# Seven of 24 attention chunks: q, k and x turned by DMAs from SBUF to SBUF instead of TensorE transposes and PSUM copies

## The chip, the cores and the metric

The kernel runs on one core of a Trainium2 chip. The time is device time in microseconds (us) of one execution. Three executions of the kernel before gave 196.27, 196.29 and 194.94 us, median 196.27. Besides, one execution was profiled; it took 197.9 us.

A core has TensorE (PE, with its weight loads shown as PEld), VectorE (DVE), ScalarE (ACT), GpSimd (POOL) and SyncE (SP), each with its own queue of instructions in a fixed order. TensorE writes into eight PSUM banks, which are emptied by DVE or ACT. DMAs move data between HBM and SBUF, or within SBUF; here all of them are issued by SP and run on 16 DMA engines.

## The reference, cut to what matters

A gated linear attention with a recurrent state, for 4 batches of 8 heads with 768 steps and a head size of 48, feeds a two-layer MLP with a squared ReLU:

```python
for t in range(S):
    state = alpha[:, :, t, :, None] * state + einsum('bhd,bhe->bhde', k[:, :, t], v[:, :, t])
    y[:, :, t] = einsum('bhd,bhde->bhe', q[:, :, t], state)
x = y.transpose(0, 2, 1, 3).reshape(3072, 384)
r = maximum(x @ w_in, 0.0)          # w_in 384 x 2048
out = (r * r) @ w_out               # w_out 2048 x 384
```

## The kernel before, in words

The 3072 tokens are 24 chunks of 128 (six per batch; a chunk of the code is `s`, its place in the batch `c`). For each chunk:

- SP loads alpha, q, k and v (L299), 192 KB each, in pieces of 192 bytes. A weight load is L264, a result's store L549.
- ACT takes the logarithm of alpha into `L_s` (L321). PE multiplies it by a triangle of ones, which gives the prefix sums (`e_p0`). ACT makes A = exp(sums) and Ainv = exp(-sums) (L340, L344) and two small decays `ae_s` (L347, L350).
- DVE makes qA_s = q * A (L359) and kI_s = k * Ainv (L362), bf16, heads padded from 48 to 64 so that two heads fill 128 columns. There are four slots of them.
- PE transposes qA_s and kI_s into a PSUM bank, four 128x128 transposes each (`e_p1q`, `e_p1k`; the helper `tr` is L224, all other matmuls are L221), and DVE copies the bank into `qkT` (`e_cp`, `cast`, L316).
- PE makes the scores `sc` from qkT (`e_p2`, 8 matmuls), DVE masks them into `sm` (L400, two halves). PE updates the state `st` (`e_ps`), DVE decays it (L420), ACT casts it to `sb` (L425).
- PE adds the part of the former state (`e_p3a`, from qkT and sb) and of the chunk itself (`e_p3b`, from sm and vb); ACT casts the bank to `xn` (L314). PE transposes xn in three blocks (`e_p4`, L224), and DVE copies them into `xT_big` (`e_xT`, L316).

The MLP runs on groups of chunks: 4, 1, 1 and then nine groups of 2. For a group, up-projection matmuls read xT_big and w_in_b, ACT applies ReLU (L504), DVE squares into `gT` (L512). Down-projection matmuls read gT and w_out_b, 16 for each chunk in four quarters; ACT or DVE copies the sum to `ob` (L544 or L542) and SP stores it.

The order of all of this is set before the kernel runs by a small planner (`Plan`). Each step is an `Op` with an engine, a cost in us, the steps it depends on, a latency until its result can be used, and the PSUM banks it takes. The planner goes through time, starts on each engine what can start first, and sorts by start. Instructions are then emitted in that order and kept in it (`pin`, `keep_in_program_order`), so every engine's queue, SP's among them, has a fixed order, and an instruction that waits holds all behind it on its engine. A store is put into the order 3.5 us after its data are planned to be there (`OUT_LATE`). `LEAD` keeps the attention some chunks ahead of the MLP, so that between the steps of a chunk PE has up- and down-projection matmuls of earlier groups.

Loads have six buffers each, `qkT`, `xn` and `sm` four.

Of the kernel before, what the change touches and what calls it, by code (L numbers as in the profile page):

```python
# [9 lines left out]
BF16 = mybir.dt.bfloat16  # L10
# [44 lines left out]
def after(op, x=0.0):  # L55
    return (op, x)
# [83 lines left out]
def kernel(  # L140
# [10 lines left out]
    nc = tc.nc  # L151
    B, H, S, D = q.shape
    HD = H * D
    P = 128
    DP = 64
    NP = H // 2
# [17 lines left out]
    big = ctx.enter_context(tc.tile_pool(name="big", bufs=1))  # L174
    LB = 6
    loads = ctx.enter_context(tc.tile_pool(name="loads", bufs=LB))
    work = ctx.enter_context(tc.tile_pool(name="work", bufs=4))
# [17 lines left out]
        out=utri_f, in_=utri_f, compare_op=ALU.is_ge, fill=0.0,  # L195
# [10 lines left out]
    NBUF = 4  # L206
    L_s = big.tile([P, NBUF, H, DP], BF16)
    nc.gpsimd.memset(L_s[:, :, :, D:], 0.0)
    qA_s = big.tile([P, NBUF, H, DP], BF16)
    nc.gpsimd.memset(qA_s[:, :, :, D:], 0.0)  # L210
    kI_s = big.tile([P, NBUF, H, DP], BF16)
    nc.gpsimd.memset(kI_s[:, :, :, D:], 0.0)
    ae_s = big.tile([P, NBUF, NP, 2], FP32)
    nc.vector.memset(ae_s, 0.0)  # L214
    xT_big = big.tile([P, KT, n_tok], BF16)

    def pin(ins):
        tc.keep_in_program_order(ins)
# [4 lines left out]
    def tr(*a):  # L223
        pin(nc.tensor.transpose(*a))  # L224

    plan = Plan()
# [4 lines left out]
    GLA_BANKS = sl_bank[0:2]  # L231
# [11 lines left out]
    def add(eng, dur, emit, *deps, **kw):  # L243
        return plan.add(Op(eng, dur, emit, deps, **kw))
# [43 lines left out]
    state = {}  # L288
    SRC = dict(srcs)
    EARLY = 4  # L290

    def add_load(s, nm):
        d = C[s]
        b, c = divmod(s, NCH)

        def ld():
            if nm not in d:
                d[nm] = loads.tile([P, H, D], FP32, name=nm)
            pin(nc.sync.dma_start(out=d[nm], in_=SRC[nm][b, c]))  # L299
        prev = C[s - LB]["use_" + nm] if s >= LB else None  # L300
        d["ld_" + nm] = add("DMA", LD, ld, prev, lat=2.0 if s < 4 else 2.4, at=0.8)

    def add_chunk(s):
        d = C[s]
        b, c = divmod(s, NCH)
        i = s % NBUF
        L, qA, kI, ae = L_s[:, i], qA_s[:, i], kI_s[:, i], ae_s[:, i]
        old = C[s - NBUF].get("end") if s >= NBUF else None
        g = dict(prio=-10.0 + s * 0.01)
        last = c == NCH - 1  # L310

        def cast(op, out_t, in_t):
            if op.eng == "ACT":
                pin(nc.scalar.copy(out_t, in_t))  # L314
            elif op.eng == "DVE":
                pin(nc.vector.tensor_copy(out_t, in_t))  # L316
            else:
                pin(nc.gpsimd.tensor_copy(out_t, in_t))

        def e_ln():  # L320
            pin(nc.scalar.activation(L[:, :, 0:D], d["at"], AF.Ln))  # L321
        ln = d["use_at"] = add("ACT", 0.41, e_ln, d["ld_at"], old, prio=-15.0 if s < EARLY else -5.0)

# [39 lines left out]
        mq = d["use_qt"] = add("DVE", 0.47, e_qA, a_, d["ld_qt"], old, **g)  # L363
        mk = d["use_kt"] = add("DVE", 0.47, e_kI, ai, d["ld_kt"], old, **g)
# [6 lines left out]
        def e_p1k():  # L371
            for p in range(NP):
                tr(d["pT"][:, NP + p, :], kI[:, 2 * p:2 * p + 2, :], ident_bf)
        p1q = plan.add(Op("PE", 0.22, e_p1q, [mq], takes=GLA_BANKS, **g))
        p1k = plan.add(Op("PE", 0.22, e_p1k, [mk, after(p1q)], lat=0.15, **g))

        def e_cp(lo, hi):
            if lo == 0:
                d["qkT"] = work.tile([P, 2 * NP, P], BF16, name="qkT")
            cast(cpk if lo else cp, d["qkT"][:, lo:hi, :], d["pT"][:, lo:hi, :])  # L380
        if s < EARLY:
            cp = add({"ACT": 0.49, "DVE": 0.34}, 0, lambda: e_cp(0, NP), p1q, **g)
            cpk = add({"DVE": 0.34, "ACT": 0.49}, 0, lambda: e_cp(NP, 2 * NP), p1k, after(cp, -9.0), **g)
        else:
            cp = cpk = add("DVE", 0.61, lambda: e_cp(0, 2 * NP), p1k, **g)
        p1q.gives = cpk

        def e_p2():
            sc = d["sc"] = ps_sc.tile([P, 2, NP, P], FP32, name="sc")
# [60 lines left out]
        xn = add("ACT", 0.36, e_xn, p3b, **g)  # L450
        (p3a or p3b).gives = xn

        def e_p4():
            d["px"] = psum(p4, [P, KT, P], BF16)
            for j in range(KT):
                tr(d["px"][:, j, :], d["xn"][:, j * P:(j + 1) * P], ident_bf)
        p4 = plan.add(Op("PE", 0.165, e_p4, [xn], takes=GLA_BANKS, lat=0.14, **g))

        def e_xT():
            cast(xT, xT_big[:, :, s * P:(s + 1) * P], d["px"])  # L460
        xT = add({"ACT": 0.36, "DVE": 0.27} if s < EARLY else "DVE", 0.27, e_xT, p4, prio=-9.0)
        d["x"] = d["end"] = xT
        p4.gives = xT

    GN = [4, 1, 1, 2, 2, 2, 2, 2, 2, 2, 2, 2]
    assert sum(GN) == NT
# [88 lines left out]
    for d in DMA_ORDER + [s for s in range(NT) if s not in DMA_ORDER]:  # L555
        if d in ("i", "o"):
            load_w(d)
        else:
            for s, nm in LOAD_ORDER.get(d, [(d, nm) for nm, _ in srcs]):
                add_load(s, nm)  # L560
            if d == 3:
                add_chunk(2)
            if d != 2:
                add_chunk(d)
# [83 lines left out]
```

## Time and profile before

| what | value |
|---|---|
| median of three executions | 196.27 us (194.94 to 196.29) |
| the profiled execution | 197.9 us, its span 196.2 us, mean granted TensorE clock 0.991 |
| PE busy | 183.9 us, 94% of the span |
| DVE, ACT, POOL busy | 130.0, 122.4, 16.3 us |
| weight loads (PEld) busy | 133.3 us |
| DMA packets of SP's queue | 107408, 29.89 MB, 74.1% of 16 engines' span |
| chain of waits by engine | PE 75%, SP's queue 9%, DMA 8%, DVE 4% |

The span is cut into 40 slices of 4.9 us; a digit is the busy share of a slice in tenths, 9 being 90% or more. Rows of groups name the line, the engine, the operation, what it writes and reads, the shapes, and how often. The chain of waits is followed back from the last instruction: at each step to what released it, or to the instruction before it on its engine. "To landing" is the time from the issue of a DMA on SP to the arrival of its data. The granted clock of PE was 1.00 after the first 45 us; before that it was 0.50 in one stretch of some 3.4 us (39.0 to 42.4 us).

### The profile page before, as it was taken

The numbers are of one execution on the slowest core, as the hardware profiler recorded it, in microseconds if no ns is written. First come the engines' busy times: TensorE is split into PE (matmuls) and PEld (weight loads), VectorE is DVE, ScalarE is ACT, GpSimd is POOL, SyncE is SP. The second block draws the span as 40 slices with busy tenths as digits, with TensorE's granted clock in tenths as the row PEclk, the third lists the DMA queues.
The fourth block names the chain that finished last, engine by engine and source line by source line (L and its number), as shares of the span: only waits on it lengthen the run. The fifth ranks groups of instructions, "written<-read, shape, count | busy, mean of one in ns | idle before, by whom it ended". The sixth has DMA issues, their size and how long they took to land.

```text
span 196.2 us, 4979 instructions
## 1 busy us (share of the span) xinstructions
PE 183.9 (94%) x1958; PEld 133.3 (68%) x1959; DVE 130.0 (66%) x277; ACT 122.4 (62%) x291; POOL 16.3 (8%) x37
## 2 busy tenths in 40 slices
PE   7888799599979999999999999999999999999991
PEld 2566554256768787867877877867868868768660
DVE  0688897725599797985786866858758767734200
ACT  3465688323988686875956856956955845718210
POOL 5110100011103021111111100110110000000000
PEclk9999999969999999999999999999999999999999
DMA  6999999999999999999999999871100110111111
GB/s 124 190 188 152 301 383 373 196 255 175 225 251 180 153 198 201 175 191 193 222 191 209 201 177 235 158 164 40 40 35 10 38 45 5 40 40 43 39 60 62
DMA packets 107431, 30.20 MB, mean 154 GB/s; under 512 B 100368, under 2 KB 106256, under 8 KB 107408
## 3 DMA queue, kind: packets, MB, share of 16 engines
q1 hardware_dynamic: 107408, 29.89, 74.1%
q8 instruction: 15, 0.25, 0.5%
q14 instruction: 8, 0.07, 0.1%
HBM read 25.17 MB, written 4.72 MB: 152 GB/s over the span
## 4 chain that ended last, share of the span: by engine, by line
PE 75%; SPq 9%; DMA 8%; DVE 4%; issue 1%; ACT 0%
PE bank L221 65%; SPq L299 8%; PE bank L224 6%; DMA wo<-in_moe_w_out_dram 4%; DMA wi<-in_moe_w_in_dram 4%; PE sc L221 3%; PE st L221 1%; DVE w_in_b L270 1%; DVE gT L512 1%; DVE sm L400 1%; SPq L264 1%; DVE w_out_b L270 0%; DVE qkT L316 0%; DVE kI_s L362 0%; ACT A L340 0%
## 5 line engine op out<-in xcount | busy, mean ns | idle before, releaser
L221 PE MATMUL bank<-xT_big,w_in_b 128*128 128x256 bf16 (+3 forms) x587 | 76.1, 270 | 0.3 <-ACT r L504 0.2
L221 PE MATMUL bank<-w_out_b,gT 128*128 128x384 bf16 x384 | 73.1, 331 | 2.2 <-DVE w_out_b L270 2.2
L504 ACT ACTIVATE r<-bank 128x512 bf16<-128x512 f32 (+2 forms) x100 | 57.5, 585 | 19.5 <-PE bank L221 16.8
L221 PEld LDWEIGHTS <-w_in_b 128*128 128x128 bf16 x588 | 49.6, 97 | 10.6 <-DVE w_in_b L270 0.5
L221 PEld LDWEIGHTS <-gT 128*128 128x128 bf16 x384 | 35.5, 99 | 22.6 <-issue 4.0
L512 DVE TENSOR_TENSOR gT<-r 128x512 bf16<-128x512 bf16 (+2 forms) x100 | 39.0, 416 | 13.9 <-ACT r L504 13.7
L400 DVE TENSOR_TENSOR sm<-sc,utri_b 128x512 bf16<-128x512 f32 x48 | 30.8, 684 | 2.9 <-PE sc L221 2.9
L544 ACT COPY ob<-bank 128x384 f32<-128x384 f32 x24 | 11.6, 482 | 25.1 <-PE bank L221 25.0
L359 DVE TENSOR_TENSOR qA_s<-qt,A 128x384 bf16<-128x384 f32 x24 | 13.3, 554 | 20.0 <-ACT A L340 20.0
L326 POOL CAST vb<-vt 128x384 bf16<-128x384 f32 x24 | 13.5, 563 | 129.3 <-DMA vt<-in_v_dram 74.7
L316 DVE COPY qkT<-bank 128x1024 bf16<-128x1024 bf16 (+1 forms) x28 | 17.1, 614 | 9.6 <-PE bank L224 9.4
L321 ACT ACTIVATE L_s<-at 128x384 bf16<-128x384 f32 x24 | 12.5, 522 | 8.2 <-DMA at<-in_alpha_dram 8.1
L221 PEld LDWEIGHTS <-qkT 64*128 64x128 bf16 (+1 forms) x272 | 10.8, 95 | 6.8 <-issue 2.1
L340 ACT ACTIVATE A<-bank 128x384 bf16<-128x384 f32 x24 | 12.0, 498 | 4.9 <-PE bank L221 4.8
L314 ACT CAST xn<-bank 128x384 bf16<-128x384 f32 x24 | 11.5, 480 | 5.2 <-PE bank L221 5.1
L362 DVE TENSOR_TENSOR kI_s<-kt,Ainv 128x384 bf16<-128x384 f32 x24 | 13.9, 579 | 0.3 <-DMA kt<-in_k_dram 0.3
L425 ACT CAST sb<-st 128x384 bf16<-128x384 f32 x20 | 9.5, 476 | 6.2 <-DVE st L420 6.0
L221 PE MATMUL bank<-warm 128*128 128x256 bf16 (+1 forms) x59 | 11.0, 317 | 1.3 <-DVE ae_s L214 1.3
L344 ACT ACTIVATE Ainv<-bank 128x384 bf16<-128x384 f32 x24 | 12.0, 500 | 0.0
L420 DVE TENSOR_TENSOR st<-st,ae_s 128x384 f32<-128x384 f32 x20 | 11.2, 558 | 0.2 <-PE st L221 0.2
L224 PE MATMUL bank<-ident_bf,kI_s 128*128 128x128 bf16 x96 | 9.3, 219 | 1.7 <-DVE qkT L316 1.7
L221 PE MATMUL bank<-vb,sm 128*128 128x48 bf16 x192 | 9.5, 184 | 1.2 <-DVE sm L400 0.7
(38 smaller groups left out, 130.4 us busy)
## 6 DMA issues: line engine op xcount, KB each, us to landing
at<-in_alpha_dram SPq DMA_DIRECT2D x24, 192.0 KB, 4.5
qt<-in_q_dram SPq DMA_DIRECT2D x24, 192.0 KB, 4.6
kt<-in_k_dram SPq DMA_DIRECT2D x24, 192.0 KB, 4.4
vt<-in_v_dram SPq DMA_DIRECT2D x24, 192.0 KB, 4.3
out_dram<-ob SPq DMA_DIRECT2D x24, 192.0 KB, 2.9
wo<-in_moe_w_out_dram SPq DMA_DIRECT2D x4, 768.0 KB, 8.7
wi<-in_moe_w_in_dram SPq DMA_DIRECT2D x3, 768.0 KB, 7.6
wi<-in_moe_w_in_dram SPq DMA_DIRECT2D x2, 384.0 KB, 5.7
```

Source lines behind the costliest of these rows:

```text
L221: pin(nc.tensor.matmul(*a, **kw))
L224: pin(nc.tensor.transpose(*a))
L299: pin(nc.sync.dma_start(out=d[nm], in_=SRC[nm][b, c]))
L316: pin(nc.vector.tensor_copy(out_t, in_t))
L321: pin(nc.scalar.activation(L[:, :, 0:D], d["at"], AF.Ln))
L326: pin(nc.gpsimd.tensor_copy(d["vb"], d["vt"]))
L340: pin(nc.scalar.activation(d["A"], d["pm"][:, 0:HD].rearrange("p (h d) -> p h d", h=H), AF.Exp))
L359: pin(nc.vector.tensor_mul(qA[:, :, 0:D], d["qt"], d["A"]))
L362: pin(nc.vector.tensor_mul(kI[:, :, 0:D], d["kt"], d["Ai"]))
L400: pin(nc.vector.tensor_mul(d["sm"][:, hh], d["sc"][:, hh], utri_b.to_broadcast([P, NP, P])))
L504: pin(nc.scalar.activation(box["r"][:, 0:w], box["ph"][:, 0:w], AF.Relu))
L512: pin(nc.vector.tensor_mul(gT[g][:, f0:f0 + per, lo * P:lo * P + n], r, r))
```

## The change

From chunk 17 on, qA_s and kI_s of a chunk, which now lie side by side in one tile `qk_s`, are transposed into qkT by one DMA from SBUF to SBUF on SP's queue, and xn is transposed into xT_big by another. The transposes on PE, their PSUM banks and the DVE copies are left out for these chunks. The planner gets a new engine "XB" for the two steps, with costs of 0.8 and 0.5 us and a latency of 2.0 us; this only sets the order, since both are issued by SP. Chunks 0 to 16 are as before.

```diff
-    qA_s = big.tile([P, NBUF, H, DP], BF16)
+    qk_s = big.tile([P, NBUF, 2, H, DP], BF16)
+    qA_s, kI_s = qk_s[:, :, 0], qk_s[:, :, 1]
     nc.gpsimd.memset(qA_s[:, :, :, D:], 0.0)
-    kI_s = big.tile([P, NBUF, H, DP], BF16)
     nc.gpsimd.memset(kI_s[:, :, :, D:], 0.0)
...
+    XFROM = 17
...
-        p1q = plan.add(Op("PE", 0.22, e_p1q, [mq], takes=GLA_BANKS, **g))
-        p1k = plan.add(Op("PE", 0.22, e_p1k, [mk, after(p1q)], lat=0.15, **g))
+        if s < XFROM:
+            p1q = plan.add(Op("PE", 0.22, e_p1q, [mq], takes=GLA_BANKS, **g))
+            p1k = plan.add(Op("PE", 0.22, e_p1k, [mk, after(p1q)], lat=0.15, **g))
...
-        if s < EARLY:
+        def e_turn():
+            d["qkT"] = work.tile([P, 2 * NP, P], BF16, name="qkT")
+            pin(nc.sync.dma_start_transpose(out=d["qkT"], in_=qk_s[:, i].rearrange("p x h d -> p (x h d)")))
+        if s >= XFROM:
+            cp = cpk = add("XB", 0.8, e_turn, mq, mk, lat=2.0, **g)
+        elif s < EARLY:
...
-        p1q.gives = cpk
+        if s < XFROM:
+            p1q.gives = cpk
...
-        p4 = plan.add(Op("PE", 0.165, e_p4, [xn], takes=GLA_BANKS, lat=0.14, **g))
+        if s < XFROM:
+            p4 = plan.add(Op("PE", 0.165, e_p4, [xn], takes=GLA_BANKS, lat=0.14, **g))
...
-        xT = add({"ACT": 0.36, "DVE": 0.27} if s < EARLY else "DVE", 0.27, e_xT, p4, prio=-9.0)
+        def e_xturn():
+            pin(nc.sync.dma_start_transpose(out=xT_big[:, :, s * P:(s + 1) * P], in_=d["xn"]))
+        if s < XFROM:
+            xT = add({"ACT": 0.36, "DVE": 0.27} if s < EARLY else "DVE", 0.27, e_xT, p4, prio=-9.0)
+            p4.gives = xT
+        else:
+            xT = add("XB", 0.5, e_xturn, xn, lat=2.0, prio=-9.0)
         d["x"] = d["end"] = xT
-        p4.gives = xT
```

## The prediction

> **What bounds the kernel now.** I read the page first, then the busy times by stretch, then the chain of waits in order of time, then the timeline of one chunk, and last the DMA queue around the place of the change. In the page's slices, two rows matter: PE, and the share of the DMA engines.
>
> ```profile
> PE   7888799599979999999999999999999999999991
> ...
> DMA  6999999999999999999999999871100110111111
> ```
>
> A slice is 4.9 us. PE is full from slice 13 to the last but one. The DMA engines are full up to slice 25 (123 us), at 8 and 7 tenths in the next two, and nearly empty from 132 us. Chunk 17's kI_s, the first product that the change sends through a DMA, ends at 126.97 us (DVE row of L362, start 126.42 us, 0.55 us), just where the loads run out. The stretch from there to the last chunk's x is this one (columns: stretch, length, busy us of PE, PEld, DVE, ACT and POOL with counts, granted clock, DMA share, GB/s):
>
> ```profile
> 126.00:176.00 50.00, 50.00 (x547) 37.52 (x545) 34.62 (x75) 31.54 (x78) 1.59 (x3) 1.00 0.18 50
> ```
>
> PE is busy 50.00 of 50.00 us at full clock and the view of waits lists none for it here. DVE and ACT have a third of their time left. So time taken off PE's queue here is time off the end, as long as no new wait takes its place. The chain of waits says how much the transposes hold (start, length, what):
>
> ```profile
> 161.30 0.17 PE bank L224 x3
> 161.47 0.65 PE bank L221 x4
> 162.12 0.45 PE bank L224 x8
> 162.57 0.17 PE st L221 x4
> 162.74 0.98 PE bank L221 x9
> 163.72 0.33 PE sc L221 x8
> ```
>
> L224 is the transpose helper: 3 matmuls for x of one chunk (0.17 us of the chain), 8 for q and k of the next (0.45 us, elsewhere as two times 0.22). Last, what a transposed chunk waits for today, from the timeline (start, length, instruction):
>
> ```profile
> 159.58 0.32 PE L221 MATMUL bank<-L_s,utri_b 128*128 128x384 bf16 x1
> ...
> 161.34 0.55 DVE L362 TENSOR_TENSOR kI_s<-kt,Ainv 128x384 bf16<-128x384 f32 x1
> ...
> 162.60 0.69 DVE L316 COPY qkT<-bank 128x1024 bf16<-128x1024 bf16 x1 [0.45 <-PE bank L224]
> ...
> 163.65 0.40 PE L221 MATMUL sc<-qkT 64*128 64x128 bf16 x8
> ```
>
> The prefix sums (L_s) start at 159.58 us, kI_s is done at 161.89 us, the scores (sc) start at 163.65 us: 1.76 us from kI_s to the scores now.
>
> **What it removes.** Seven chunks (17 to 23) lose 4+4+3 transposes each. On the chain 0.17+0.45 = 0.61 to 0.62 us a chunk, so 7 x 0.61 = 4.3 us off PE. This is the whole possible gain: -4.3 us. (The busy times of the 77 matmuls add to 7.23 us, but they overlap each other; the chain's share counts.) DVE loses 7 qkT copies of 0.69 and 7 xT copies of 0.35 us, 7.3 us: costed at nothing, since DVE's 15.4 us of idle time in the stretch hide it; no wait of PE's ends in it, so without that cover there would still be no gain. Two PSUM banks come free sooner; no wait here is for a bank: nothing. q and k now share one tile, with the same memsets: nothing.
>
> **What it adds.** Per chunk two DMAs on SP's queue: q and k together (128x1024 bf16, 256 KB), x (128x384, 96 KB). By their output shapes (128x8x128, 128x3x128) I count 1024 and 384 pieces of 256 B, 64 and 24 for each of 16 DMA engines. No row shows such a DMA. Its neighbours are loads (1024 pieces of 192 B) and results (128 pieces of 1536 B), issue to landing. In the stretch where the loads run out, and in the quiet one after it:
>
> ```profile
> qt<-in_q_dram SPq DMA_DIRECT2D x1, 192.0 KB, 2.9
> kt<-in_k_dram SPq DMA_DIRECT2D x1, 192.0 KB, 3.5
> vt<-in_v_dram SPq DMA_DIRECT2D x1, 192.0 KB, 3.7
> ```
>
> ```profile
> out_dram<-ob SPq DMA_DIRECT2D x10, 192.0 KB, 1.9
> ```
>
> The lower end is 1.9 us. The upper is the median of loads in a crowd, 4.4 us (page, kt). I take 2.9 us: qt had the rings almost to itself and has the 64 pieces per engine that q and k have, while kt and vt, issued 0.5 and 1.1 us behind it, queued on it. With 0.03 us from a finished producer to SP's issue (ob ends at 160.05, its result is issued at 160.08 us) and some 0.1 us (estimate of the same kind) to PE, the way from kI_s to the scores is L = 3.03 us; ends 2.0 and 4.5.
>
> **Who waits for it.** PE runs in a fixed order, so scores that are late hold everything behind them. The changed order puts them later. Counting what PE does from a chunk's prefix sums to its scores in that order (three up-projection matmuls 0.33, four down-projection 0.65, scores 0.33, state 0.17, p3a 0.17, p3b 0.21, prefix sums 0.26 us, all from the timeline): 5.7, 6.0, 5.6, 5.7, 5.4, 5.7, 5.6 us for chunks 17 to 23. From prefix sums to the end of kI_s the trace takes 2.3 us (159.58 to 161.89), or 2.5 where a ReLU lies between (166.74 to 169.27); I take 2.4. The rooms for L are 3.3, 3.6, 3.2, 3.3, 3.0, 3.3, 3.2 us, 22.9 in sum. At L = 3.03 nothing waits but chunk 17: its DMA stands behind qt of chunk 23 in the rings, which was issued at 126.53 and landed 2.9 us later, at 129.4 us. Then come 64 pieces per engine at 21.7 ns (74.1% of 16 engines' 196.2 us over 107408 packets), 1.4 us, so 130.8 us against 126.97+3.3 = 130.3: +0.6 us with the hop.
>
> Moved on SP: chunk 17's transpose stands ahead of kt and vt of chunk 23, which are needed 30 us later; x of chunks 19 and 21 stands ahead of q and k of 20 and 22, issued some 0.3 us before kI_s is done (p3b starts 1.08 us after the prefix sums, xn ends 1.05 us later, kI_s at 2.4), and 24 pieces at 21.7 ns, 0.5 us, go first: 0.15 us each, +0.3 us. Results between them have left ACT long before (they are ordered 3.5 us late). x itself: xn ends some 1.05 us after its chunk's p3b starts (159.38 to 160.43 us), and from p3b to the group's first up-projection PE has 5.0 us of work for chunk 17 (whose x stands behind q and k of 18) and 4.1 to 4.3 us for 19, 21 and 23: rooms of 3.9 and 3.1 to 3.2 us. Its landing lies between the result's 1.9 and qt's 2.9 us, so nothing; if it took 4.4 us, about 1.3 us for each of three groups.
>
> **The sum.** -4.3 +0.6 +0.3 = -3.4 us. The profiled execution took 197.9 us, 1.7 us more than its span of 196.2; by the sum it would take 194.5 us. The three runs shown have a median of 196.27 us, 0.8% below it; the terms are differences within the span, so I set them against this median: 192.9 us.
>
> [...] The row: SP needs 0.33 us for a result's issue and 0.37 us for qt's. [...]
>
> **Rivals.**
> *Slower, SP's issue or the crossbar is slow.* If a transpose lands later than the scores' turn, PE stands still in each chunk. For: SP's longest issue of a load took 2.51 us (vt at 121.98); against: that one met full rings. With 2.5 us of issue and the 1.6 us that a result needs after its issue, L = 4.2: six chunks wait 6 x 4.2 - 19.6 = 5.6, chunk 17 waits 0.9, x ahead of q and k costs 0.6 twice. -4.3+7.7 = +3.4 us, 199.7 us. The loads in a crowd, L = 4.5, give +8.6-4.3, 200.6 us. It decides from 6L - 19.6 + 0.6 = 4.3, L = 3.9 us.
> *A wash.* L of 3.5 to 4.1 us (kt's and vt's 3.5 and 3.7 us are such rows): waits of 1.5 to 5.0 us in chunks 18 to 23, 0.6 to 0.8 in 17, 0.3 for x: -1.9 to +1.8 us, 194.4 to 198.1 us.
> *Block by block.* If the eight 128-column blocks pass one after another, each like a small DMA, a block costs up to a result's 1.9 us: L up to 15.3 us, 7 x 15.3 - 22.9 - 4.3 = +80 us, 276 us; with half of that L, +26 us, 222 us. Nothing in the trace speaks for it, and nothing excludes it. [...]
>
> **How the numbers follow.** Forecast, L up to 3.5 us: 0.42, 192.9 us, own range 192.0 (no wait at all) to 194.4. Wash: 0.18. Slow issue or landing, 198 to 204 us: 0.25. Block by block, above 204 us: 0.15. That leaves 0.40 on the slow side, since no row shows this kind of DMA and the room is only some 0.3 us wider than the row I take. About 1% (2 us) is what can be told from no change. Faster 0.44 (the forecast and the wash's lower edge), same 0.16, slower 0.40. The range reaches from 192.0 to 204 us (L = 5.0: 7 x 5.0 - 22.9 - 4.3 = +7.8), beyond the crowded loads and short of the last case.
>
> **What would show it.** After: L224 gone past 127 us; PE's busy share in the stretch still 100% and the mean distance between two chunks' scores (now 129.33 to 171.63 us, six steps, 7.05 us) at 6.4 us; one wait of sc on a DMA of about 0.6 us, in chunk 17; transposes landing 2.9 us after issue. Wrong: a wait of sc on qkT's DMA in every chunk (rivals one or three), SP rows of over 1 us for a transpose (issue), or waits of the up-projection on xT_big's DMA.

## The result and the profile after

Median after the change 194.51 us (193.08 to 195.72, 20 runs), before it 196.19 us (194.92 to 198.40, 20 runs). The ratio is 0.9929, interval 0.9904 to 0.9953: the change gains 1.4 us (0.9 to 1.9), 0.7%. Ratios, here and below, compare the fast executions alone and are not exactly the ratio of the two medians, which differ by 1.7 us here. The forecast was a gain of 3.4 us. The direction was right, and less than half of the size came.

The profiled execution after has a span of 192.6 us, 3.6 less than the one before. That is more than the medians differ, because the one before lost some time ahead of the change: its first step of chunk 17 (qA_s, L359) began at 125.96 us, the one after had it at 124.18. In the former, PE's clock was 0.50 from 39.0 to 42.4 us; in the latter it was not there, only past 191 us at the very end. So I compare stages: from the start of chunk 17's qA_s to the end of the last copy to ob it is 66.77 us before and 65.10 after, 1.7 us less, which is about what the medians say. The first and last step of this stage (start, length), before:

```profile
125.96 0.55 DVE L359 TENSOR_TENSOR qA_s<-qt,A 128x384 bf16<-128x384 f32 x1
...
192.25 0.48 ACT L544 COPY ob<-bank 128x384 f32<-128x384 f32 x1 [2.12 <-PE bank L221]
```

and after, where qA_s is a half of qk_s:

```profile
124.18 0.55 DVE L360 TENSOR_TENSOR qk_s<-qt,A 128x384 bf16<-128x384 f32 x1
...
188.80 0.48 ACT L558 COPY ob<-bank 128x384 f32<-128x384 f32 x1 [2.12 <-PE bank L221]
```

Where the 4.3 us of relief went is seen in the same views as before. The stretch from 126 to 176 us of the profile after (length, busy us of PE, PEld, DVE, ACT, POOL with counts, clock, DMA share, GB/s):

```profile
126.00:176.00 50.00, 47.51 (x479) 33.82 (x477) 27.23 (x56) 30.49 (x74) 1.79 (x3) 1.00 0.44 100
```

PE was busy for all of these 50 us before, now for 47.51. It idles 2.5 us, and the waits say for what; in PE's timeline after, all waits of the stretch end at the scores (start, length, instruction, in brackets the idle time and its releaser):

```profile
129.31 0.40 PE L221 MATMUL sc<-qkT 64*128 64x128 bf16 x8 [0.83 <-DMA qkT<-qk_s]
...
135.75 0.40 PE L221 MATMUL sc<-qkT 64*128 64x128 bf16 x8
...
141.78 0.40 PE L221 MATMUL sc<-qkT 64*128 64x128 bf16 x8
...
149.29 0.40 PE L221 MATMUL sc<-qkT 64*128 64x128 bf16 x8 [0.99 <-DMA qkT<-qk_s]
...
155.57 0.40 PE L221 MATMUL sc<-qkT 64*128 64x128 bf16 x8
...
163.01 0.40 PE L221 MATMUL sc<-qkT 64*128 64x128 bf16 x8 [0.60 <-DMA qkT<-qk_s]
...
169.32 0.40 PE L221 MATMUL sc<-qkT 64*128 64x128 bf16 x8
```

Chunks 17, 20 and 22 wait, 0.83+0.99+0.60 = 2.4 us; 18, 19, 21 and 23 do not. 4.3 - 2.4 = 1.9 us is what is left. The transposes land about as fast as was forecast, 2.9 us for q and k (all seven chunks, median us from issue to landing):

```profile
qkT<-qk_s SPq DMA_TRANSPOSE x7, 3.2
xT_big<-xn SPq DMA_TRANSPOSE x7, 2.3
```

But SP's own timeline shows what no row of before could: issuing one transpose holds SP for 1.2 us or more. Before, a result's issue took 0.33 us and a load's where the loads run out 0.37 (the first row gives the least, the median and the longest issue in ns):

```profile
L549 SPq DMA_DIRECT2D out_dram<-ob x16: 332/332/942, 105.1 to 192.8; - x16
...
126.53 0.37 SPq L299 DMA_DIRECT2D qt<-in_q_dram  x1
```

After:

```profile
144.50 1.57 SPq L471 DMA_TRANSPOSE xT_big<-xn  x1
146.17 1.26 SPq L385 DMA_TRANSPOSE qkT<-qk_s  x1
147.52 0.53 SPq L563 DMA_DIRECT2D out_dram<-ob  x1
```

kI_s of chunk 20 was done at 145.08 us (DVE, start 144.22, 0.86 us). SP was then in the middle of issuing x of chunk 19 and came to q and k only at 146.17, 1.1 us late. They landed 3.1 us later, and PE waited 0.99 (a result's issue behind a transpose takes some 0.5 us now, as in the last row). In chunk 22 it was the same: x of chunk 21 was issued from 158.62 to 159.80 us, kI_s was done at 158.90, q and k were issued at 159.91, 1.0 us late, and PE waited 0.60. In chunk 19, with SP free, the issue came 0.07 us after kI_s (138.40 to 138.47 us), and nobody waited.

### The profile page after: what moved, and what is told of

It is laid out like the page before. It is cut to its first block, busy times and chain, and to the rows that moved or that the text cites. A ratio compares the mean times of both kernels' runs of the same rounds, so it can differ in the third digit from the quotient of the medians.

```text
span 192.6 us, 4840 instructions
## 1 busy us (share of the span) xinstructions
PE 178.5 (93%) x1881; PEld 128.7 (67%) x1882; DVE 124.6 (65%) x263; ACT 122.2 (63%) x291; POOL 16.2 (8%) x37
## 4 chain that ended last, share of the span: by engine, by line
PE 70%; DMA 12%; DVE 9%; ACT 4%; issue 2%; SPq 1%; DVEq 0%; ACTq 0%
PE bank L221 60%; DMA qkT<-qk_s 7%; PE bank L224 5%; DMA wo<-in_moe_w_out_dram 4%; PE sc L221 4%; DVE qkT L317 2%; DVE sm L408 2%; DMA at<-in_alpha_dram 2%; PE st L221 1%; ACT r L518 1%; DVE gT L526 1%; DVE qk_s L363 1%; DVE w_in_b L270 1%; SPq L471 1%; ACT A L341 1%
## 5 line engine op out<-in xcount | busy, mean ns | idle before, releaser
L221 PE MATMUL bank<-xT_big,w_in_b 128*128 128x256 bf16 (+3 forms) x587 | 75.3, 270 | 1.0 <-ACT r L518 0.9
L221 PE MATMUL bank<-w_out_b,gT 128*128 128x384 bf16 x384 | 70.4, 326 | 1.0 <-DVE w_out_b L270 1.0
L526 DVE TENSOR_TENSOR gT<-r 128x512 bf16<-128x512 bf16 (+2 forms) x100 | 40.4, 424 | 18.2 <-ACT r L518 18.0
L360 DVE TENSOR_TENSOR qk_s<-qt,A 128x384 bf16<-128x384 f32 x24 | 13.3, 555 | 14.5 <-ACT A L341 14.5
L317 DVE COPY qkT<-bank 128x1024 bf16<-128x1024 bf16 (+1 forms) x21 | 12.2, 586 | 6.9 <-PE bank L224 6.8
L363 DVE TENSOR_TENSOR qk_s<-kt,Ainv 128x384 bf16<-128x384 f32 x24 | 14.4, 601 | 0.0
L224 PE MATMUL bank<-ident_bf,qk_s 128*128 128x128 bf16 x136 | 12.1, 219 | 2.1 <-DVE qkT L317 1.7
L221 PE MATMUL bank<-warm 128*128 128x256 bf16 (+1 forms) x59 | 11.9, 338 | 1.3 <-DVE ae_s L214 1.3
L221 PE MATMUL sc<-qkT 64*128 64x128 bf16 x192 | 9.5, 219 | 3.0 <-DMA qkT<-qk_s 2.4
L224 PEld LDWEIGHTS <-qk_s 128*128 128x128 bf16 x136 | 9.5, 98 | 4.2 <-issue 1.0
```

Source lines behind the costliest of these rows:

```text
L221: pin(nc.tensor.matmul(*a, **kw))
L360: pin(nc.vector.tensor_mul(qA[:, :, 0:D], d["qt"], d["A"]))
L363: pin(nc.vector.tensor_mul(kI[:, :, 0:D], d["kt"], d["Ai"]))
L526: pin(nc.vector.tensor_mul(gT[g][:, f0:f0 + per, lo * P:lo * P + n], r, r))
```

## Experiments

Theory: the rest of the gain is lost where two transposes are due on SP at once (chunks 20 and 22), and where a transpose stands behind loads (chunk 17). Rivals: the transposes land too late by themselves; the order on SP is merely wrong; part of the gain comes from elsewhere.

**One transpose alone.** For q and k alone, `e_p4` and its copy stay on PE and DVE for all chunks; for x alone, the same with `e_p1q`, `e_p1k` and their copy:

```diff
-        if s < XFROM:
+        if True:
             p4 = plan.add(Op("PE", 0.165, e_p4, [xn], takes=GLA_BANKS, lat=0.14, **g))
```

> From chunk 17 on only q and k go through a DMA; x is transposed on TensorE again. Theory (SP needs about 1.2 us to issue a transpose, and the waits of the scores in chunks 20 and 22 come from x being issued ahead of q and k): the scores wait on qkT only in chunk 17 (about 0.8 us), PE is relieved of 7 x 0.45 = 3.1 us, so -2.3 us against before, 193.9 us, faster than the change as made by half a microsecond although it moves less. Rival (q and k land too late by themselves, x in front of them does not matter): waits of 0.6 to 1.0 us in chunks 20 and 22 stay, 2.4 us in sum, so -0.7 us, 195.5 us.

> From chunk 17 on only x goes through a DMA; q and k stay on TensorE. Theory: x lands 2.3 us after its issue, inside its room of 3.1 us or more, so PE waits for nothing and is relieved of 7 x 0.17 = 1.2 us: 195.0 us against 196.2 before. Rival (the DMA of x has a price of its own, through its landing or what it holds up on SP): waits of the up-projection on xT_big's DMA, 196 us or more.

q and k alone: 193.76 us (4 runs), ratio 0.9853 (0.9809 to 0.9897). The waits of PE are these:

```profile
128.88 0.40 PE L221 MATMUL sc<-qkT 64*128 64x128 bf16 x8 [0.56 <-DMA qkT<-qk_s]
...
135.10 0.40 PE L221 MATMUL sc<-qkT 64*128 64x128 bf16 x8 [0.18 <-DMA qkT<-qk_s]
...
161.63 0.40 PE L221 MATMUL sc<-qkT 64*128 64x128 bf16 x8 [0.28 <-DMA qkT<-qk_s]
```

1.0 us in all; chunk 20's wait is gone and chunk 22's is halved without an x ahead of them. Moving less gained no less. x alone: 193.98 us (4 runs), ratio 0.9868 (0.9836 to 0.9899), no wait of PE from 100 us on; its stage is 1.3 us shorter, as expected, but its median fell by more, 2.4 us. What made that excess is open; one program measured in two sets (the planner's costs, below) differs by 1.3 us, more than the excess of 1.1. Its two profiled executions began chunk 17 at 123.40 and at 125.32 us with stages of the same length, so at least in these two the difference lies ahead of the change.

**The order on SP.** x of chunks 19 and 21 is moved behind q and k of 20 and 22, on SP alone:

```diff
+    for s_ in (19, 21):
+        x = C[s_]["x"]
+        t = min((o for o in plan.order if o.eng == "XB" and o.start > x.start), key=lambda o: o.start)
+        plan.order.remove(x)
+        plan.order.insert(plan.order.index(t) + 1, x)
```

> As the change, but on SP's queue x of chunks 19 and 21 stands behind q and k of chunks 20 and 22 instead of ahead of them; every other engine's order is the same. Theory (1.2 us of SP's time per transpose is the price, and two transposes are due at once): the waits of the scores in chunks 20 and 22 (0.99 and 0.60 us) go, and waits of about 0.9 and 0.6 us of the up-projection on x take their place, since x lands 1.2 us later against a room of some 0.3 us; time as with the change, 194.5 us. Rival (only the order on SP is wrong): the waits go and nothing takes their place, 193 us.

195.58 us (12 runs) against 196.88 before on that chip: 0.9918 (0.9887 to 0.9948), not told apart from the change. The waits of chunks 20 and 22 only changed their place. In PE's timeline:

```profile
148.86 0.49 PE L221 MATMUL bank<-xT_big,w_in_b 128*128 128x256 bf16 x3 [1.26 <-DMA xT_big<-xn]
...
155.66 0.40 PE L221 MATMUL sc<-qkT 64*128 64x128 bf16 x8 [0.16 <-DMA qkT<-qk_s]
...
162.93 0.49 PE L221 MATMUL bank<-xT_big,w_in_b 128*128 128x256 bf16 x3 [0.76 <-DMA xT_big<-xn]
```

Now the up-projection waits for x, 1.26 and 0.76 us. It is SP's time that is short, not its order that is wrong.

**What the issue depends on.** q and k get a DMA each, 128x512, which is 32 tiles of 16x128, counted by shape alone (q and k together are 64, x is 24):

```diff
-            cp = cpk = add("XB", 0.8, e_turn, mq, mk, lat=2.0, **g)
+            cp = add("XB", 0.4, lambda: e_turn(0), mq, lat=2.0, **g)
+            cpk = add("XB", 0.4, lambda: e_turn(1), mk, after(cp, -9.0), lat=2.0, **g)
```

> As the change, but q and k are transposed by a DMA each, 32 tiles of 16x128 in place of 64; q's is issued when q is ready, 0.5 us ahead of k. It asks what SP's issue time depends on; with the change it is 1.24 us for 64 tiles and 1.18 us for 24. If it is a price per instruction: 1.2 us for each, SP busy 3.6 us a chunk, q and k complete 0.2 to 0.5 us later than with the change, in chunks 20 and 22 some 1.2 us later, about 196 us. If it goes by tiles or pieces: about 0.6 us for each, q and k complete 0.5 us earlier, the waits of chunks 17, 20 and 22 shrink, about 193.5 us.

SP's timeline at chunk 19, its two issues in one row (with the gap of 0.09 us between them) and then an x's:

```profile
141.13 2.50 SPq L386 DMA_TRANSPOSE qkT<-qk_s  x2
143.72 1.21 SPq L473 DMA_TRANSPOSE xT_big<-xn  x1
```

In the trace 24 tiles (x) take 1.21 us, 32 tiles 1.19 and 1.22, and 64 took 1.24 with the change (lowest 1.23): between these sizes the price is per instruction. In proportion to the 1.24 us of 64 tiles, 24 and 32 would by an estimate take 0.47 and 0.62 us; the measurement decides against it. The time is 201.07 us (4 runs), 1.0188 (1.0130 to 1.0246), much more than the 196 expected. The waits sum to 6.1 us, 1.8 more than the relief. A further part, in the profiled execution, is PE's clock. After the wait of 1.43 us in chunk 20 (to 154.00 us) the stretches read:

```profile
152.50:154.00 1.50, 0.07 (x2) 0.01 (x2) 0.00 (x0) 0.00 (x0) 0.00 (x0) 1.00 0.57 141
154.50:157.50 3.00, 3.00 (x28) 2.27 (x27) 2.63 (x5) 1.70 (x4) 0.00 (x0) 0.50 0.01 3
```

The granted clock is halved for some 3.4 us right after the wait, which costs 1.7 us more; 0.7 us of the 4.2 by which the stage is longer stay unexplained. The halving followed 1.43 us of waiting, with another 0.23 us 0.5 us before it; in other runs single waits of 1.45 and 1.53 us were not followed by it (last section), and one of this kernel's four executions, the fastest with 199.24 us, has a mean clock of 1.000.

**Among the loads.** `XFROM = 9` instead of 17.

> The change begins at chunk 9 instead of 17, so that the transposes of chunks 9 to 16 share the 16 DMA engines with the loads. Theory (in a crowd a transpose stands behind what is in the rings, as chunk 17's did behind one load): landing of 4.5 us or more after the issue, waits of about 1.5 to 2.5 us in each of these chunks, 8 x 2 = 16 us against 8 x 0.61 = 4.9 us of relief, about 205 us; the loads come later too. Rival (SP's issue is the whole price and the rings' fill does not matter): the waits of chunks 9 to 16 are as those of 18 to 23, 0 to 1 us, and the time falls to about 191 to 193 us.

210.53 us (4 runs), 1.0728 (1.0673 to 1.0783), 5 us beyond the 205 expected. Landing, the cause that I had named, is the smaller part. From 80 to 140 us q and k took 3.8 us to land, 0.6 more than the 3.2 in the quiet. What is late above all is the issue: in chunks 10 to 16 it comes 0.6 to 3.3 us after kI_s, because SP is still issuing loads, an x or a result. SP's timeline in chunk 12, whose kI_s was done at 91.12 us:

```profile
90.70 1.97 SPq L300 DMA_DIRECT2D at<-in_alpha_dram  x1
92.78 1.76 SPq L385 DMA_TRANSPOSE qkT<-qk_s  x1
```

The load's issue is long here, 1.97 us; whether the busy DMA engines made it so or a fetch of instructions that began at 90.81 us (such fetches come up below) is not shown.

PE's waits are 12.9 us on q and k and 3.8 on x, against 15 x 0.61 = 9.2 us of relief. Two stretches at half clock of some 6.8 us each (from 97 and from 131 us) add about 6.8. Together +14.3 us; measured +14.1.

**The planner's costs.** The planner had put too small an issue into the order, so I gave it the measured ones:

```diff
-            cp = cpk = add("XB", 0.8, e_turn, mq, mk, lat=2.0, **g)
+            cp = cpk = add("XB", 1.3, e_turn, mq, mk, lat=2.0, **g)
...
-            xT = add("XB", 0.5, e_xturn, xn, lat=2.0, prio=-9.0)
+            xT = add("XB", 1.25, e_xturn, xn, lat=1.15, prio=-9.0)
```

> As the change, but the planner is told what the trace shows: 1.3 us of SP's time for q and k and 2.0 us after it, 1.25 us for x and 1.15 us after it (instead of 0.8 and 0.5 us, each with 2.0). Nothing else differs; PE's order shifts. Theory (the missing gain is lost to orders that are built on too short an issue): waits on qkT fall from 2.4 us to at most 1 us, in chunk 17 alone, and the time to about 193 us. Rival (the waits are of the DMA itself, or something other than PE's waits eats the gain): the sum of waits stays near 2.4 us, or it falls and the time stays near 194.5 us.

194.02 us (4 runs), 0.9861 (0.9822 to 0.9899). Against the theory, 2.0 us of waits stayed, in two other chunks, 18 (0.46) and 20 (1.53), although SP was free for both. In PE's timeline:

```profile
133.94 0.40 PE L221 MATMUL sc<-qkT 64*128 64x128 bf16 x8 [0.46 <-DMA qkT<-qk_s]
...
147.07 0.40 PE L221 MATMUL sc<-qkT 64*128 64x128 bf16 x8 [1.53 <-DMA qkT<-qk_s]
```

Their transposes landed 4.2 and 4.1 us after the issue instead of 3.1. In chunk 20 the new order adds to it: without the wait the scores' turn would come 2.7 us after kI_s, too soon even for a landing after 3.1 us.

> The kernel with the planner's true costs (1.3 us on SP and 2.0 after it for q and k, 1.25 and 1.15 for x) once more, on the same chip as the version with shifted fetches, for a comparison of the two. Theory: waits on qkT at chunks 18 and 20 again, where the fetches fall, time 1.0 to 1.4% below the kernel before. Rival (their place is chance from run to run): waits at other chunks or none.

The same program on another chip gave 195.21 us (10 runs), 0.9929 (0.9904 to 0.9955), and the same two waits, 0.53 and 1.45 us. So their place is the program's, not chance. The DMA view of the window from 145.0 to 149.2 us, 40 slices of 0.1 us, holds chunk 20's transpose, issued at 145.00 us:

```profile
DMA  0000000006049999999000000006999900000699
GB/s 0 0 0 0 0 0 0 0 0 156 0 85 212 212 207 205 185 100 27 0 7 7 10 10 10 10 10 127 283 285 295 286 3 0 0 0 12 137 207 224
...
q8 instruction: 1, 0.02, 1.7%
```

Half of the data come at some 200 GB/s. Then for 0.8 us only 7 to 10 GB/s move, and then the second half flows. In the window lies one packet of 16 KB of an instruction queue (q8), a fetch of instructions by DMA. The trace's single packets show it from 145.97 us on for 1.16 us, and the longest 256-byte piece of this transpose took 1.22 us instead of 0.02. As I read it, the engine that is fetching held up its piece, and with it the whole transpose.

The profile of the change has such packets too, from 120 to 171 us one every 12.0 to 12.8 us, with 228 to 267 of PE's matmuls and weight loads between two of them (252 on average from 15 to 170 us). Two of them began while SP was issuing a transpose: at 132.06 us in the issue for chunk 18, which took 1.71 us, and at 144.65 us in the issue of chunk 19's x, the 1.57 us shown above. The other issues of transposes from 133 us on took 1.18 to 1.26 us. So by an estimate (1.57 us less some 1.22) 0.35 us of chunk 20's wait of 0.99 comes from a fetch; this was not tested apart.

**Moving the fetches.** On top of the true costs, the filler matmuls at the start (on zeros, ahead of the real work) are cut narrower, at nearly the same total width; that puts 132 more instructions on PE, all ahead of chunk 4:

```diff
-    for _ in range(7):
-        mm(wp, lhsT=warm[:, 0:P], rhs=warm, start=True, stop=True)
+    for _ in range(21):
+        mm(wp[:, 0:170], lhsT=warm[:, 0:P], rhs=warm[:, 0:170], start=True, stop=True)
...
-                for _ in range(n):
-                    mm(wp[:, 0:256], lhsT=warm[:, 0:P], rhs=warm[:, 0:256], start=True, stop=True)
+                for _ in range(2 * n):
+                    mm(wp[:, 0:128], lhsT=warm[:, 0:P], rhs=warm[:, 0:128], start=True, stop=True)
```

> As the kernel with the planner's true costs (1.3 and 2.0, 1.25 and 1.15 us), but the filler matmuls on zeros that keep TensorE running at the start are cut into more and narrower ones of the same total width: 66 more matmuls, 132 more instructions on PE, all before chunk 4. It moves the places where 16 KB of PE's instructions are fetched by DMA (every 256 instructions, some 12.7 us here) by about 6.6 us against the attention's steps. In the profile of the kernel with true costs the two late transposes (chunks 18 and 20, landing 4.2 and 4.1 us after issue) began while such a fetch held one of the 16 DMA engines. Theory (those two waits, 0.46 and 1.53 us, come from the fetch): no wait of PE on a transpose of chunks 18 to 23 except where a fetch now falls, 1.5 to 2 us less than the kernel with true costs, about 192 to 193 us. Rival (they come from something else at that place): waits at chunks 18 and 20 as before, same time.

192.99 us (5 runs), 0.9825 (0.9792 to 0.9858), 2.2 us less than the true costs alone on the same chip. PE waits twice, in chunks 17 and 20:

```profile
130.30 0.40 PE L221 MATMUL sc<-qkT 64*128 64x128 bf16 x8 [0.56 <-DMA qkT<-qk_s]
...
147.31 0.40 PE L221 MATMUL sc<-qkT 64*128 64x128 bf16 x8 [0.53 <-DMA qkT<-qk_s]
```

Chunk 20 waits 0.53 us instead of 1.45. The window of its transpose (144.1 to 148.3 us, 0.1 us a slice) now has no 16 KB packet and no hole; the transpose lands after 3.1 us, and what is left of the wait is the distance of 2.7 us in this order:

```profile
DMA  0000000000006999999999892000000000000299
```

Chunk 18 no longer waits, but chunk 17 waits 0.56 us in its place: a fetch (125.58 to 126.94 us) now falls into its issue among the loads, which takes 2.82 us, and chunk 18's turn comes later by that wait. So the gain in waits, 0.9 us, is chunk 20's. Relief less waits, 4.3 - 1.1 = 3.2 us, is what the stage gained, 66.77 to 63.56 us, 1.0 us more than with the true costs alone; the rest of the 2.2 us lies outside the stage.

**Controls.** Two kernels without any transposing DMA (`XFROM = 99`): the first has only the tile shared by q and k, the second the narrower fillers as well:

> No chunk is transposed by a DMA; all that is left of the change is that q and k share one tile. Every engine's order is that of the kernel before. It asks whether a part of the measured gain comes from elsewhere, because the profiled runs with the change reach chunk 17 some 1.8 to 2.6 us earlier than the profiled run before, whose half-clock stretch near 40 us they do not have. Theory (the tile's layout does nothing; that stretch is chance): 196.2 us, within 0.4% of the kernel before. Rival (the layout, or the memsets that differ with it, speeds up the early part): about 1 to 1.5 us less than before, 195 us, so that the DMA transposes themselves gain little or nothing.

> The narrower fillers at the start without any transposing DMA: a control for the version with shifted fetches. Theory (cutting the fillers changes nothing by itself; what it gained came from the transposes that no longer meet a fetch): the kernel before's time, within 0.3%. Rival (part of that gain is the fillers' own, in the time ahead of chunk 17): 0.4 to 0.6% below.

196.84 us (12 runs), 1.0001 (0.9974 to 1.0027), and 196.49 us (12 runs), 0.9990 (0.9961 to 1.0018). Neither the layout nor the fillers do anything by themselves that these intervals of 0.3% show. The first one's profile has a span of 194.4 us, no half clock, and reaches chunk 17 at 124.25 us: the half-clock stretch in the profile before, and with it the 125.96 us, were chance.

**More room.** Two more versions let the attention run further ahead: `LEAD` 4.0 with 1.3 + 2.4 us for q and k (0.6 more in chunk 17) and 1.25 + 1.3 for x; and `LEAD` 3.75 with 1.3 + 2.2 us for q and k alone.

> As the change, with costs in the planner that leave room for a late landing (q and k 1.3 us on SP and 2.4 after it, 0.6 more for chunk 17; x 1.25 and 1.3) and the attention allowed half a chunk further ahead of the MLP, so that PE has work of other groups for the longer distance. Theory (the gain is lost in waits for the DMA, all of which a longer distance hides): no wait of PE on a transpose after chunk 17, the whole 4.3 us of relief less at most 0.5, 192.2 us. Rival (the longer distance costs PE work or other waits): PE waits elsewhere, 194 us or more.

> Only q and k go through a DMA from chunk 17 on (x stays on TensorE), with 1.3 us on SP and 2.2 us after it in the planner, and the attention allowed a quarter of a chunk further ahead. Theory (a transpose DMA that has SP to itself and 3.5 us of PE's work ahead of its user costs nothing, save where a load or a fetch of instructions holds an engine): 3.1 us of relief less 0 to 1 us, 1.1 to 1.6% below the kernel before, as much as with x moved too. Rival (the further lead costs more than it covers): 0.7% or less below.

With both moved: 195.62 us (12 runs), 0.9913 (0.9881 to 0.9945). PE waits twice, 1.05 us in chunk 18, whose transpose now stands behind the four last loads and lands 5.2 us after its issue, and 1.18 us in chunk 20, one of whose pieces took 1.9 us with a fetch in the same window and which also lands after 5.2 us. The 192.2 us expected were not reached. With q and k alone: 194.21 us (6 runs), 0.9874 (0.9837 to 0.9911), within the 1.1 to 1.6% expected, and no wait on a transpose at all.

Relief less waits against the stage, for the kernels with the lead of before that change chunks 17 to 23 or none (us; the stage is the one from chunk 17's qA_s to the last ob):

| kernel | relief | waits | relief less waits | stage shorter by | ratio |
|---|---|---|---|---|---|
| the change | 4.3 | 2.4 | 1.9 | 1.7 | 0.9929 |
| q and k alone | 3.1 | 1.0 | 2.1 | 1.7 | 0.9853 |
| x alone | 1.2 | 0 | 1.2 | 1.3 | 0.9868 |
| x behind q and k on SP | 4.3 | 2.7 | 1.6 | 1.1 | 0.9918 |
| q and k in a DMA each | 4.3 | 6.1 | -1.8 | -4.2 | 1.0188 |
| true costs, two sets | 4.3 | 2.0, 2.0 | 2.3, 2.3 | 2.3, 2.2 | 0.9861, 0.9929 |
| true costs, fetches moved | 4.3 | 1.1 | 3.2 | 3.2 | 0.9825 |
| no DMA | 0 | 0 | 0 | 0.0 | 1.0001 |

But for q and k in a DMA each, where 1.7 us of halved clock come on top, the stages follow within 0.5 us. The ratios of the sets with 4 runs scatter by some 0.7% (the two of one program), so they do not rank the first three rows.

## Why the prediction fell short

- *The bound* was right: PE was full, and 0.61 us a chunk could be taken off it. L224 is gone from the changed chunks, PE idles only for the waits on transposes, and where nothing waited the stage shortened by the relief (x alone: 1.3 us for 1.2).
- *The landing* was about right, and partly by luck: 2.9 us taken, 3.2 measured, x 2.3 between the ends of 1.9 and 2.9. The 2.9 us of qt were 0.37 us of issue and 2.5 after it; the transposes of q and k in chunks 19 to 23 took 1.23 to 1.26 and then 1.8 to 2.0 us. A longer issue and a shorter rest nearly made up for each other. The pieces took 21.4 ns in the trace's packets, the estimate from the loads was 21.7.
- *The rooms* were right: chunks 18, 19, 21 and 23 do not wait with 3.2 us to landing, as rooms of 3.0 to 3.6 us allow; from kI_s to the scores' turn the trace shows 3.2 to 3.8 us.
- *The step that failed* is "x of chunks 19 and 21 stands ahead of q and k of 20 and 22 ... 0.15 us each, +0.3 us". It counted x's 24 pieces on the DMA engines, 0.5 us, and had no term for SP's own time, as if an issue took no longer than qt's 0.37 us. The issue takes 1.2 us (1.57 for chunk 19's x), so q and k of chunks 20 and 22 were issued 1.1 and 1.0 us late, and the waits were 0.99 and 0.60, 1.6 us in place of 0.3. That it is SP's time was tested: without x on SP chunk 20's wait went, and with x behind q and k the waits went over to x. Chunk 17's term was 0.6 and measured 0.83; why was not tested apart. With 2.4 us of waits for 0.9, the sum becomes -1.9 us; measured -1.4 (-0.9 to -1.9). The mean distance between two chunks' scores became (169.32 - 129.31) / 6 = 6.67 us, not 6.4, and the sign of being wrong that came was "SP rows of over 1 us for a transpose".
- *The rivals*: "SP's issue is slow" named the mechanism and the place (x ahead of q and k, at 0.6 us each), but priced it at 2.5 us an issue with a late landing too, and so on the slow side. The wash had the right size for the wrong reason, a longer landing. "Block by block" is excluded: all eight blocks are in after 3.2 us. The vt issue of 2.51 us at 121.98 us, put down to full rings there, has a 16 KB fetch of instructions within it (122.12 to 123.35 us in the trace before); what held it is not shown.

## What to carry to other kernels

Moving work from the busy engine to a DMA moves it onto the issuing queue too: count that queue's time per instruction (1.2 us for a transpose here), above all where two instructions become due together, and give the planner the measured number. A DMA that feeds an engine running in a fixed order needs a distance for its latest landing, not its median: here 3.2 us in the quiet, up to 5.2 beside a fetch of instructions or behind loads. In one run TensorE's clock was 0.50 for 3.4 us after a wait of 1.43 us, in two others it stayed at 1.00 after 1.45 and 1.53 us, so a late landing may cost more than its own length.

## What the runs showed of the hardware

- Issuing a transposing DMA held SP for 1.2 us or more at the three sizes run (at the lowest 1.18 us for 24 tiles, 1.19 for 32, 1.23 for 64), against 0.33 us for a result's and 0.37 for qt's before.
- Instructions are fetched by DMA too, in packets of 16 KB (15 of them in the profile before, 0.5% of 16 engines' span). Such a fetch took 0.9 to 1.4 us in the profiles before and after. Where it met a transpose's data, the transpose landed 4.0 to 5.2 us after its issue instead of 3.1; where it began within an issue, the issue took 1.57 or 1.71 us in the change. Two profiled executions of one program had the late landings at the same two chunks.
- PE's clock was halved for 3.4 us after a wait of 1.43 us (q and k in a DMA each) and for 6.8 us after waits of 1.4 to 1.7 us close together (`XFROM = 9`), but not after single waits of 1.45 and 1.53 us in two other runs. Which gap halves it was not settled.
